# Top-k attention and an exact-GELU MLP in one kernel: an earlier first load, fewer zero products, and the first MLP block spread over two slots

## The chip, the cores and the metric

One core of one Trainium2 chip runs the whole kernel. The metric is device time in microseconds (us), the median of repeated executions. A NeuronCore has five engines that each run their own instruction stream and wait for one another through semaphores: TensorE (PE in the profile, its weight loads PEld), VectorE (DVE), ScalarE (ACT), GpSimd (POOL) and SyncE (SP, which here only issues transfers).

## The reference, cut to what matters

```python
# q, k, v: (8, 8, 576, 64) float32; w_in: (512, 2048); w_out: (2048, 512)
scores = scale * np.matmul(q, k.transpose(0, 1, 3, 2))          # scale = 1/8
kth = np.partition(scores, -top_k, axis=-1)[..., -top_k:-top_k + 1]   # top_k = 32
scores = np.where(scores >= kth, scores, -1000000000.0)
attn = np.exp(scores - scores.max(-1, keepdims=True))
attn = attn / (attn.sum(-1, keepdims=True) + 1e-09)
x = np.matmul(attn, v)        # then (B, H, S, D) -> (4608 tokens, 512)
h = x @ w_in
g = 0.5 * h * (1.0 + erf(h / sqrt(2)))
out = g @ w_out
```

For each of 64 heads, each of 576 queries keeps its 32 largest of 576 scores, a softmax over those, and the product with v. The 4608 x 512 result goes through a two-layer MLP with an exact GELU.

## The kernel before

Two heads form a pair. A pair's 576 queries are cut into 4 tiles of 128 rows and a rest of 64 rows a head. One **slot** handles one such tile for both heads; there are 144 slots and four more to drain the pipeline. The stages of a tile are spread over slots: in slot n the kernel computes the scores of tile n + 2, the top-k of tile n, the softmax of tile n - 1, the transposes of tile n - 2 and the product with v (attend) of tile n - 3. VectorE does the top-k: four rounds of MAX8 with MATCH_REPLACE8 between them, for two heads.

From slot 10 on, MLP work is put between, in **pieces**. A piece is two products of 256 columns for the first layer (l1) or one of 512 columns for the second (l2). There are 1152 pieces in all, in blocks of eight, taken in a fixed order: two l1 blocks first, then l2 and l1 blocks by turns. A Gelu for two units is due after every second block.

Setup and head:

```python
    raws = {n: [const.tile([P, NJ, 2, D], f32, name=f"raw_{n}{i}") for i in range(m)]
            for n, m in (("k", 2), ("q", 2), ("v", NP + 1))}
    for n, ts in raws.items():
        for t in ts[: 1 if n == "v" else 2]:
            (nc.vector if n == "v" else nc.gpsimd).memset(t[:, NM], 0.0)
    make_identity(nc, ident)
    for t in raws["v"][1:]:
        nc.gpsimd.memset(t[:, NM], 0.0)
    # ...
    def load(n, pair, queue=None, queue2=None):
        # ...
        for e in range(2):
            queue.dma_start(
                out=t[:, 0:NM, e, :], in_=src[b, h0 + e, 0:SM].rearrange("(t p) d -> p t d", p=P)
            )
            queue2.dma_start(out=t[e * TL : (e + 1) * TL, NM, e, :], in_=src[b, h0 + e, SM:S])
    # ... memsets of low, high and ptt on GpSimd ...
    load("k", 0, nc.scalar, nc.gpsimd)
    load("q", 0)
    load("k", 1)
    load("q", 1)
    for n in range(2):
        load_weights(FIRST + n)

    idle = raws["v"][0][:, NM].rearrange("p e d -> p (e d)")
    warm = ps.tile([P, 512], f32, tag="l1", name="warm")
    for _ in range(WARM):                 # WARM = 16
        nc.tensor.matmul(warm[:, 0:P], lhsT=idle, rhs=idle, start=True, stop=True)
    for pair in range(2):
        for piece in transpose_qk(pair, pair == 0):
            piece()
        if pair == 0:
            scores(0)
            scores(1)
```

The rows NM of each raw tile hold the last 64 rows of two heads on a diagonal; the rest of them is zero, hence the memsets. The zero products write a tile that nobody reads. Each `transpose_qk` makes three groups of transposes: k's four main blocks first, then the two last blocks of q and k, then q's four main blocks; each group is copied from PSUM to SBUF (for pair 0 the first two by VectorE, the third by ScalarE). The score tile's eviction:

```python
    def scores(i):
        # ... products into t_ps (128 columns) and s_ps (2 x 512 columns) ...
            nc.scalar.activation(spread(s, S + TL, SM), s_ps, func=AF.Copy, scale=scale)
            nc.scalar.activation(s[:, SM : S + TL], t_ps[:, 0:P], func=AF.Copy, scale=scale)
```

The slot loop:

```python
    def mlp(n):
        for _ in range(n):
            if done[0] >= len(pieces) or pieces[done[0]][0] > ready[0] or left[0] == 0:
                return
            pieces[done[0]][1]()
            done[0] += 1
            left[0] -= 1
    # ...
    for n in range(ahead):

        left[0] = 7 if START < n < START + 2 * NP else 8      # START = 10, NP = 4
        weights_add(unit_in(n))
        scores(n + 2)
        product = attend(n - 3)
        # ... mlp(1) between the softmax halves and the transposes of older tiles ...
        run_gelus()
        mlp(left[0])
        run_gelus()
        if n < N:
            top_k(n, {3: lambda: inverse(n - 1)})
        # ...
        threshold(n)
        normalise(n - 1, ...)           # on VectorE, GpSimd or both
        weights_size(unit_in(n + 1))
        # ... loads for later slots ...
```

In slots 1 to 15 and 17 a unit of weights is also rebuilt from its loaded words: ScalarE's part is `weights_size`, GpSimd's is `weights_add`. A Gelu that is due runs at the next `run_gelus()`, which stands at the end of a slot and before the first piece of each l1 unit. ScalarE needs another table for Gelu than for Exp, so each Gelu brings two table loads.

Of the kernel before, what the change touches and what calls it, by code (L numbers as in the profile page):

```python
# [14 lines left out]
def kernel(  # L15
# [19 lines left out]
    nc = tc.nc  # L35
    f32, i32, u32 = mybir.dt.float32, mybir.dt.int32, mybir.dt.uint32
    bf16, i16, u16 = mybir.dt.bfloat16, mybir.dt.int16, mybir.dt.uint16
    AF = mybir.ActivationFunctionType
    ALU = mybir.AluOpType

    B, H, S, D = q.shape
    P = 128
# [3 lines left out]
    NP = H // 2  # L46
    NM = S // P
    SM = NM * P
    TL = S - SM
# [6 lines left out]
    scale = 1.0 / float(D) ** 0.5  # L56
# [8 lines left out]
    ident = const.tile([P, P], f32, name="ident")  # L65
# [4 lines left out]

    raws = {n: [const.tile([P, NJ, 2, D], f32, name=f"raw_{n}{i}") for i in range(m)]
            for n, m in (("k", 2), ("q", 2), ("v", NP + 1))}
    for n, ts in raws.items():
        for t in ts[: 1 if n == "v" else 2]:
            (nc.vector if n == "v" else nc.gpsimd).memset(t[:, NM], 0.0)
    make_identity(nc, ident)
    for t in raws["v"][1:]:
        nc.gpsimd.memset(t[:, NM], 0.0)


    n_pairs = B * NP
# [2 lines left out]
    def raw_of(n, pair):  # L84
        return raws[n][pair % len(raws[n])]

    def load(n, pair, queue=None, queue2=None):
        if pair >= n_pairs:
            return
        queue = queue or nc.sync  # L90
        queue2 = queue2 or queue
        b, h0 = pair // NP, 2 * (pair % NP)
        t, src = raw_of(n, pair), sources[n]
        for e in range(2):
            queue.dma_start(
                out=t[:, 0:NM, e, :], in_=src[b, h0 + e, 0:SM].rearrange("(t p) d -> p t d", p=P)
            )
            queue2.dma_start(out=t[e * TL : (e + 1) * TL, NM, e, :], in_=src[b, h0 + e, SM:S])

# [20 lines left out]
    ORDER = [0, 1, 2, 3, 8, 9, 4, 5, 10, 11, 6, 7, 12, 13, 14, 15]  # L122
    FIRST = 1
    START = 2 * NP + 2
    WARM = 16
    words = {}
    low = const.tile([P, 1], f32, name="low")
    nc.gpsimd.memset(low, -EXP0 * 2.0**19)
# [51 lines left out]
    def on_pool(u):  # L180

        return SLOT_OF[u] >= START
# [3 lines left out]
    def weights_add(u):  # L186
        if u in words:
            w, _, below, d = parts(u)
            if on_pool(u):
                nc.gpsimd.tensor_scalar(  # L190
                    w.bitcast(i32), w.bitcast(u32), 2.0**-13, None, op0=ALU.mult
                )
            nc.gpsimd.tensor_tensor(d, d, below, op=ALU.add)
            nc.gpsimd.tensor_tensor(d, d, w.bitcast(i32), op=ALU.add)
        made.add(u)
# [53 lines left out]
    def spread(t, step, n):  # L249

        return bass.AP(tensor=t.tensor, offset=t.offset, ap=[list(t.ap[0]), [step, 2], [1, n]])

    def half(r, e):


        return slice((r ^ e) * TL, ((r ^ e) + 1) * TL)
# [5 lines left out]
    def scores(i):  # L262
        if i >= N:
            return
        pair, t = items[i]
        S_of[i] = s = work.tile([P, 2 * S], f32, tag="s", bufs=5, name="s")
        s_ps = ps.tile([P, 2, 512], f32, tag="s", bufs=1, name="s_ps")
        t_ps = ps.tile([P, 512], f32, tag="tp", name="t_ps")
        if t < NM:
            qk = qk_of[pair]  # L270
            lhsT = qk[:, t * P : (t + 1) * P]
            nc.tensor.matmul(t_ps[:, 0:P], lhsT=lhsT, rhs=qk[:, SM + P : KT], start=True, stop=True)  # L272
            for c in range(2):
                for e in range(2):
                    rows = slice(e * D, (e + 1) * D)
                    nc.tensor.matmul(  # L276
                        s_ps[:, e, c * 256 : (c + 1) * 256], lhsT=lhsT[rows, :],
                        rhs=qk[rows, KT + c * 256 : KT + (c + 1) * 256], start=True, stop=True,
                    )
            nc.scalar.activation(spread(s, S + TL, SM), s_ps, func=AF.Copy, scale=scale)  # L280
            nc.scalar.activation(s[:, SM : S + TL], t_ps[:, 0:P], func=AF.Copy, scale=scale)  # L281
        else:
            for r in range(2):
                qk = qk_of[pair + r]
                for e in range(2):
                    nc.tensor.matmul(
                        t_ps[half(r, e), r * TL : (r + 1) * TL],
                        lhsT=qk[:, SM + e * TL : SM + (e + 1) * TL],
                        rhs=qk[:, SM + P + e * TL : SM + P + (e + 1) * TL],
                        start=True, stop=True,  # L290
                    )

            for r in range(2):
                qk = qk_of[pair + r]
                for e in range(2):
                    rows = slice(e * D, (e + 1) * D)
                    nc.tensor.matmul(  # L297
                        s_ps[half(r, e), r, :], lhsT=qk[rows, SM + e * TL : SM + (e + 1) * TL],
                        rhs=qk[rows, KT:], start=True, stop=True,
                    )  # L300
            s2 = s.rearrange("p (r n) -> p r n", r=2)
            nc.scalar.activation(s2[:, :, 0:SM], s_ps, func=AF.Copy, scale=scale)
            nc.scalar.activation(
                s2[:, :, SM:S], t_ps[:, 0:P].rearrange("p (r n) -> p r n", r=2),
                func=AF.Copy, scale=scale,
            )
# [38 lines left out]
    def inverse(i):  # L345
        if i < 0 or i >= N:
            return
        st = stat_of[i]
        nc.vector.reciprocal(st["rden"], st["den"])  # L349

    def add_small(i):
        if i < 0 or i >= N:
            return
        st = stat_of[i]
        nc.gpsimd.tensor_scalar(st["den"], st["den"], 1e-9, None, op0=ALU.add)  # L355

    def softmax(i, e):

        if i < 0 or i >= N:
            return  # L360
        st, s = stat_of[i], row(i, e)
        nc.scalar.activation(s, s, func=AF.Prelu, bias=st["neg"][:, e, 1:2], scale=1.0, alpha=STEEP)  # L362
        nc.scalar.activation(  # L363
            s, s, func=AF.Exp, bias=st["bias"][:, e : e + 1], scale=1.0,
            accum_out=st["den"][:, e : e + 1],
        )
# [58 lines left out]
    def attend(i):  # L425
# [37 lines left out]
        if t == (NM if b % 2 == 0 else NM - 1):  # L463
            for r in range(2 if t == NM else 1):
                load("v", pair + r + NP + 1)
# [93 lines left out]
    def run_gelus():  # L559
        while waiting:  # L560
            gelus(waiting.pop(0))
# [9 lines left out]
# [9 lines that stand above are left out]
    ready, left = [0], [0]  # L580
    staging = ExitStack()
    stage = staging.enter_context(tc.tile_pool(name="stage", bufs=1))

    load("k", 0, nc.scalar, nc.gpsimd)
    load("q", 0)
    load("k", 1)
    load("q", 1)
    for n in range(2):
# [4 lines left out]
    warm = ps.tile([P, 512], f32, tag="l1", name="warm")  # L593
    for _ in range(WARM):
        nc.tensor.matmul(warm[:, 0:P], lhsT=idle, rhs=idle, start=True, stop=True)  # L595
# [19 lines left out]
    ahead = N + 4  # L615
    for n in range(ahead):

        left[0] = 7 if START < n < START + 2 * NP else 8
        weights_add(unit_in(n))
        scores(n + 2)  # L620
        product = attend(n - 3)
        late = n > START
        mlp(1)
        tr = transposes(n - 2)
        if product and n > START and done[0] < len(pieces) and pieces[done[0]][0] > ready[0]:

            for piece in tr[:1]:
                piece()
            tr, ready[0] = tr[1:], n_tok[0]
        softmax(n - 1, 0)  # L630
        mlp(1)
        if not late:
            softmax(n - 1, 1)
        mlp(1)
        prep = prep_in.pop(n, [])
        if len(prep) > 1 and len(tr) == 3:
            tr, prep = tr[:1] + prep[:1] + tr[1:], prep[1:]
        for piece in tr[:-1]:
            piece()
            ready[0] = n_tok[0]  # L640
            mlp(1)
        ready[0] = n_tok[0]
        if late:
            softmax(n - 1, 1)
        add_small(n - 1)
        for piece in tr[-1:] + prep:
            piece()
            mlp(1)
# [6 lines that stand above are left out]
        else:  # L655
            inverse(n - 1)
        threshold(n)
        u = unit_in(n + 1)

        normalise(n - 1, 0 if u not in words else 2 if on_pool(u) else 1)  # L660

        weights_size(unit_in(n + 1))
        if n >= FIRST:
            load_weights(n + 2)
        if n <= NP:
            load("v", n)
# [38 lines left out]
```

## Time and profile before

| what | value |
|---|---|
| median of 3 executions | 1654.69 us (1654.48 to 1655.39) |
| span of the profiled execution | 1653.7 us |
| TensorE busy | 1593.8 us |
| VectorE busy | 1419.6 us |
| ScalarE busy | 1184.1 us |
| GpSimd busy | 650.5 us |
| mean granted TensorE clock | 0.977 of full |
| MAX8, one instruction | 746 ns, 1152 of them |

A row of the page's second part cuts the span into 40 slices of 41 us; a digit is the busy share in tenths. In a timeline row, "xN" means that N instructions of one kind were merged; the bracket is the idle time of the engine before the row, with the instruction that ended it. A matrix product of float32 shows as two records a product, a transpose as one.

### The profile page before, as it was taken

To read this page: it belongs to the slowest core of one execution; us is meant where nothing else is said; L and a number is where in the kernel's file an instruction comes from. 1 tells how busy PE (TensorE), PEld (TensorE's weight loads), DVE (VectorE), ACT (ScalarE), POOL (GpSimd) and SP (SyncE) were. 2 spreads that over 40 slices of the span, in tenths; PEclk is the share of its full clock that TensorE was granted. 3 is DMA by queue.
4 is the path that set the end of the run, shared out by engine and by line. 5 is a ranking of instruction groups with operands and counts; after the bars stand their busy time and mean duration, and the time that the engine had idled before them with its cause. 6 is when DMAs were issued, how large, how long until landed. Compare 5 with 4: busy or idle time off the path is not lost.

```text
span 1653.7 us, 25056 instructions
## 1 busy us (share of the span) xinstructions
PE 1593.8 (96%) x8832; PEld 1080.5 (65%) x8832; DVE 1419.6 (86%) x3049; ACT 1184.1 (72%) x2131; POOL 650.5 (39%) x756
## 2 busy tenths in 40 slices
PE   6669999999999999999999999999999999999999
PEld 4346566766666667676666667676666666666665
DVE  7999899989999889998989988998889898999800
ACT  6888777777777777777777777777777777777720
POOL 3677543333333333333333333333333333333300
PEclk7669999999999999999999999999999999999999
DMA  6423210011101111011110111001110001000000
GB/s 165 139 98 102 83 43 1 14 29 29 50 1 28 30 30 28 1 28 36 29 28 1 42 29 43 1 14 28 44 35 1 27 15 34 2 14 4 4 13 13
DMA packets 126621, 56.14 MB, mean 34 GB/s; under 512 B 117760, under 2 KB 117792, under 8 KB 126496
## 3 DMA queue, kind: packets, MB, share of 16 engines
q1 hardware_dynamic: 125376, 54.25, 12.2%
q8 instruction: 70, 1.15, 0.3%
q14 instruction: 55, 0.45, 0.1%
q10 hardware_dynamic: 1056, 0.26, 0.1%
q0 software_dynamic: 64, 0.03, 0.0%
HBM read 45.08 MB, written 9.44 MB: 33 GB/s over the span
## 4 chain that ended last, share of the span: by engine, by line
PE 92%; ACT 6%; DVE 1%; issue 1%; POOL 0%; ACTq 0%; POOLq 0%; DVEq 0%
PE h_ps L495 30%; PE y_ps L531 30%; PE o L443 9%; PE s_ps L276 8%; PE tp L412 8%; PE tp_qk L231 2%; PE t_ps L272 2%; ACT s L363 1%; PE o L454 1%; ACT s L362 1%; PE s_ps L297 1%; PE tp_t L394 1%; ACT s L280 1%; POOL s L375 0%; PE warm L595 0%
## 5 line engine op out<-in xcount | busy, mean ns | idle before, releaser
L323 DVE MAX8 top<-rest 128x8 f32<-128x576 f32 x864 | 608.9, 746 | 0.0
L495 PE MATMUL h_ps<-xT,w_in_sb 128*128 128x256 f32 (+1 forms) x2560 | 554.5, 362 | 3.8 <-ACT g L506 3.8
L531 PE MATMUL y_ps<-w_out_sb,g 128*128 128x512 f32 x1152 | 549.5, 599 | 0.0
L495 PEld LDWEIGHTS h_ps<-xT,w_in_sb 128*128 128x128 f32 x2560 | 429.6, 191 | 66.6 <-issue 19.6
L375 POOL TENSOR_SCALAR s<-s,rden 128x576 f32<-128x576 f32 x266 | 456.0, 1723 | 0.8 <-issue 0.4
L326 DVE MATCH_REPLACE8 rest<-top,rest 128x576 f32<-128x576 f32 x576 | 423.0, 741 | 0.0
L355 POOL TENSOR_SCALAR den<-den 128x2 f32<-128x2 f32 x144 | 32.0, 222 | 835.2 <-ACT s L363 834.4
L531 PEld LDWEIGHTS y_ps<-w_out_sb,g 128*128 128x128 f32 x1152 | 195.1, 190 | 166.8 <-issue 165.0
L280 ACT ACTIVATE s<-s_ps 128x1024 f32<-128x1024 f32 x128 | 131.5, 1027 | 167.3 <-PE s_ps L276 149.1
L363 ACT ACTIVATE s<-s,bias 128x576 f32<-128x576 f32 x288 | 223.3, 776 | 13.3 <-ACT s L362 0.7
L362 ACT ACTIVATE s<-s,neg 128x576 f32<-128x576 f32 x288 | 223.9, 778 | 0.3 <-POOL neg L338 0.2
L419 ACT COPY pt<-tp 128x512 f32<-128x512 f32 x256 | 147.1, 574 | 103.0 <-PE tp L412 103.0
L412 PEld LDWEIGHTS tp<-ident,s 128*128 128x128 f32 x1152 | 145.9, 144 | 111.9 <-issue 59.1
L326 DVE MATCH_REPLACE8 rest<-top,s 128x576 f32<-128x576 f32 x288 | 211.6, 742 | 0.0
L323 DVE MAX8 top<-s 128x8 f32<-128x576 f32 x288 | 201.8, 742 | 3.9 <-ACT s L281 3.9
L412 PE MATMUL tp<-ident,s 128*128 128x128 f32 x1152 | 178.6, 279 | 23.6 <-ACT pt L395 22.0
L443 PE MATMUL o<-pt,raw_v 128*64 128x256 f32 x1280 | 155.5, 390 | 0.0
L276 PE MATMUL s_ps<-qk 64*128 64x256 f32 x1024 | 153.9, 421 | 0.7 <-ACT s L280 0.7
L349 DVE RECIPROCAL rden<-den 128x2 f32<-128x2 f32 x144 | 23.0, 160 | 142.1 <-POOL den L355 141.8
L443 PEld LDWEIGHTS o<-pt,raw_v 128*64 128x64 f32 x1280 | 87.8, 139 | 66.2 <-issue 23.4
L276 PEld LDWEIGHTS s_ps<-qk 64*128 64x128 f32 x1024 | 92.5, 195 | 23.7 <-issue 1.6
L506 ACT ACTIVATE g<-h_ps 128x512 f32<-128x512 f32 x144 | 78.6, 595 | 34.0 <-PE h_ps L495 33.2
(66 smaller groups left out, 1088.3 us busy)
## 6 DMA issues: line engine op xcount, KB each, us to landing
raw_q<-in_q_dram SPq DMA_DIRECT2D x64, 128.0 KB, 2.4
raw_v<-in_v_dram SPq DMA_DIRECT2D x64, 128.0 KB, 2.5
out_dram<-y SPq DMA_DIRECT2D x32, 256.0 KB, 2.1
w_out_sb<-in_moe_w_in_dram SPq DMA_DIRECT2D x16, 511.8 KB, 4.9
raw_k<-in_k_dram SPq DMA_DIRECT2D x62, 128.0 KB, 2.5
w_out_sb<-in_moe_w_out_dram SPq DMA_DIRECT2D x10, 511.8 KB, 3.9
words<-in_moe_w_out_dram SPq DMA_DIRECT2D x6, 511.8 KB, 4.5
raw_q<-in_q_dram SPq DMA_DIRECT2D x64, 16.0 KB, 2.3
```

The costliest lines, as they stand in the source:

```text
L276: nc.tensor.matmul(s_ps[:, e, c * 256 : (c + 1) * 256], lhsT=lhsT[rows, :], rhs=qk[rows, KT + c * 256 : KT + (c + 1) * 256], start=True, s ...
L280: nc.scalar.activation(spread(s, S + TL, SM), s_ps, func=AF.Copy, scale=scale)
L323: nc.vector.max(st["top"][:, e, 8 * r : 8 * r + 8], cur[e])
L326: nc.vector.match_replace(rest[:, e], st["top"][:, e, 8 * r : 8 * r + 8], cur[e], LOWEST)
L362: nc.scalar.activation(s, s, func=AF.Prelu, bias=st["neg"][:, e, 1:2], scale=1.0, alpha=STEEP)
L363: nc.scalar.activation(s, s, func=AF.Exp, bias=st["bias"][:, e : e + 1], scale=1.0, accum_out=st["den"][:, e : e + 1],)
L375: (nc.vector if e >= 2 - on_dve else nc.gpsimd).tensor_scalar(s, s, st["rden"][:, e : e + 1], None, op0=ALU.mult)
L412: nc.tensor.transpose(tp[:, j * P : (j + 1) * P], s[:, first + j * P : first + (j + 1) * P], ident)
L419: nc.scalar.copy(out=dst, in_=tp.rearrange("p (j n) -> p j n", j=NM))
L443: nc.tensor.matmul(o[e * D : (e + 1) * D, 0:n], lhsT=vt[:, j, e, :], rhs=pt[:, e * NM + j if j < NM else 2 * NM, :], start=(j == 0), stop= ...
L495: nc.tensor.matmul(h_tile(u)[:, i, :], lhsT=w_in_sb[:, ko, f * P : (f + 1) * P], rhs=xT[:, ko, c0 : c0 + n], start=(ko == 0), stop=(ko == ...
L531: nc.tensor.matmul(y_of[sub], lhsT=g_of[u][:, i, sub * P : (sub + 1) * P], rhs=w_out_sb[:, f, :], start=(f == 0), stop=(f == FT - 1),)
```

## The change

It has four parts, all at the start of the kernel.

- The first tile's rows NM of k are cleared first, by GpSimd, and the loads of k and q for pair 0 are issued right after it, before the identity is made. The other memsets of raw tiles go to VectorE. This is to have k's last rows, which GpSimd loads, in place sooner.
- Nine zero products run instead of sixteen.
- Of the first score tile, ScalarE evicts only one half of s_ps; VectorE evicts t_ps and the other half.
- Slots 10 and 11 take four MLP pieces each instead of eight and seven, and slots 12 to 17 take eight instead of seven. The first l1 block thus spans slots 10 and 11, and from slot 12 on each slot takes exactly one block.

```diff
-    for n, ts in raws.items():
-        for t in ts[: 1 if n == "v" else 2]:
-            (nc.vector if n == "v" else nc.gpsimd).memset(t[:, NM], 0.0)
-    make_identity(nc, ident)
-    for t in raws["v"][1:]:
-        nc.gpsimd.memset(t[:, NM], 0.0)
+    nc.gpsimd.memset(raws["k"][0][:, NM], 0.0)
+    for t in raws["v"][:1] + raws["q"] + raws["k"][1:] + raws["v"][1:]:
+        nc.vector.memset(t[:, NM], 0.0)
 # ... after the definition of load():
+    load("k", 0, nc.scalar, nc.gpsimd)
+    load("q", 0)
+    make_identity(nc, ident)
 # ...
-    WARM = 16
+    WARM = 9
 # ... in scores(), for a tile of 128 rows:
+            if i == 0:
+
+                nc.scalar.activation(s[:, 0:SM], s_ps[:, 0], func=AF.Copy, scale=scale)
+                nc.vector.tensor_scalar(s[:, SM : S + TL], t_ps[:, 0:P], scale, None, op0=ALU.mult)
+                nc.vector.tensor_scalar(s[:, S + TL :], s_ps[:, 1], scale, None, op0=ALU.mult)
+                return
             nc.scalar.activation(spread(s, S + TL, SM), s_ps, func=AF.Copy, scale=scale)
 # ... before the zero products:
-    load("k", 0, nc.scalar, nc.gpsimd)
-    load("q", 0)
     load("k", 1)
     load("q", 1)
 # ... at the top of the slot loop:
-        left[0] = 7 if START < n < START + 2 * NP else 8
+        left[0] = 4 if n in (START, START + 1) else 8
```

## The prediction

> **What bounds the kernel now.** I read the page first: the engine totals, the forty slices and the chain that ended last.
>
> ```profile
> PE 1593.8 (96%) x8832; PEld 1080.5 (65%) x8832; DVE 1419.6 (86%) x3049; ACT 1184.1 (72%) x2131; POOL 650.5 (39%) x756
> PE   6669999999999999999999999999999999999999
> DVE  7999899989999889998989988998889898999800
> PEclk7669999999999999999999999999999999999999
> PE 92%; ACT 6%; DVE 1%; issue 1%; POOL 0%; ACTq 0%; POOLq 0%; DVEq 0%
> ```
>
> TensorE is full from the fourth slice (41 us each) to the end, and 92% of the chain is TensorE. Only the first three slices, 0 to about 124 us, show it at 6. The last two slices are TensorE alone: MLP pieces left over after the last attention slot. So a microsecond is gained only if TensorE reaches its saturated stretch earlier with the same number of pieces done, and such a microsecond reaches the end whole.
>
> Next the timeline, first at the start and then where the Gelus run.
>
> ```profile
> 1.04 6.67 PE L595 MATMUL warm<-raw_v 128*128 128x128 f32 x32 [1.04 <-DVE raw_v L75]
> 2.73 1.26 POOL L98 DMA_DIRECT2D raw_k<-in_k_dram  x2
> 7.55 0.60 PE L231 MATMUL tp_qk<-ident,raw_k 128*128 128x128 f32 x4
> 11.86 1.02 ACT L280 ACTIVATE s<-s_ps 128x1024 f32<-128x1024 f32 x1 [1.65 <-PE s_ps L276]
> 12.78 0.27 ACT L281 ACTIVATE s<-t_ps 128x128 f32<-128x128 f32 x1
> 13.09 1.42 DVE L323 MAX8 top<-s 128x8 f32<-128x576 f32 x2 [3.88 <-ACT s L281]
> ...
> 180.77 1.74 PE L495 MATMUL h_ps<-xT,w_in_sb 128*128 128x256 f32 x4 [2.66 <-ACT g L506]
> 187.19 0.17 DVE L349 RECIPROCAL rden<-den 128x2 f32<-128x2 f32 x1 [4.04 <-POOL den L355]
> ```
>
> Columns: start, duration, engine, line, operation, and in brackets the idle time before it and what ended it. The first top-k starts at 13.09 us. From there VectorE has no idle row until slot 11: the first MAX8 of slots 1 to 11 stand at 22.74, 33.01, 43.28 and so on to 115.87 (slot 10) and 126.64 (slot 11), 10.27 us apart and 10.77 where it also does both normalisations. So the first 126 us are a VectorE chain hanging from 13.09. At 180.77 TensorE stands 2.66 us for a Gelu, and VectorE pays 4.04 us for it at 187.19.
>
> Then I cut the time at the first score product of each slot on TensorE, for slots 11 to 17.
>
> ```profile
> 127.59:137.72 10.13, 9.26 (x53) 7.46 (x52) 8.95 (x20) 9.56 (x16) 7.12 (x5) 1.00 0.67 229
> 137.72:148.51 10.79, 10.79 (x59) 6.33 (x58) 10.68 (x23) 8.73 (x16) 8.79 (x7) 1.00 0.07 22
> 148.51:160.46 11.95, 9.83 (x49) 6.62 (x47) 10.89 (x24) 11.78 (x19) 8.96 (x8) 1.00 0.18 69
> 160.46:172.45 11.99, 11.65 (x72) 7.11 (x71) 10.64 (x23) 9.12 (x17) 8.78 (x6) 1.00 0.47 138
> 172.45:187.36 14.91, 11.47 (x53) 7.25 (x53) 10.78 (x24) 12.27 (x20) 8.86 (x7) 0.89 0.37 110
> 187.36:199.15 11.79, 11.66 (x76) 7.87 (x76) 9.80 (x21) 6.84 (x15) 4.07 (x6) 1.00 0.01 1
> 199.15:206.79 7.64, 7.64 (x37) 3.75 (x38) 7.55 (x16) 7.48 (x12) 7.31 (x5) 1.00 0.35 78
> ```
>
> Columns after the stretch: its length, busy time of PE, PEld, DVE, ACT, POOL, then clock, DMA share and GB/s. Slot 15 (172.45) takes 14.91 us for 11.47 us of TensorE work, at a mean clock of 0.89. Slot 18 starts at 206.79.
>
> **What the Trainium skill says.** *TensorE: Matmul & The Clock Gate*, section "Part 1: The HAM clock gate": TensorE starts at half clock and is released after one busy window of about 3.4 us; the windows run freely, so the moment varies from run to run. The trace agrees: the sixteen zero products take 6.4 us up to the first transpose at 7.43, 0.40 us each, and the eight score records take 1.14 us at full clock (10.68) against 2.08 at half (17.87). The clock digit of the first 7 us carries no record; it isn't evidence of full clock. *ScalarE: Activation LUTs*, "What ACT_TABLE_LOAD costs": about 1.28 us for the load and 1.38 for a drain. The trace has the 1.28 (at 178.73) but the Gelu starts 0.02 us after it, so I count 1.28. *PSUM — Partial Sum Buffer*, "PSUM bank collisions raise a hardware error": two engines may read different banks at once. The two halves of s_ps are two banks, so the split of the first scores can overlap; no pair of this kind is in the trace before.
>
> **The change, part by part.**
>
> *Head.* Seven zero products less: 7 x 0.40 = 2.8 us, so the first transpose could start at 7.43 - 2.80 = 4.63. What it needs: k's main rows, issued at 0.72 and 1.24 on ScalarE's queue and landing 2.9 and 3.4 later, at 3.6 and 4.64; the identity, which now follows two DMA issues on GpSimd (1.26 us) and is there before 3. So 4.70. The second group needs q's last rows (issued 2.48, 2.7 to land: 5.2) and k's last rows: before, these were issued at 2.73 and 3.5 and landed at 6.0, which would have been the next bound; now the issue follows one memset (0.92), about 1.8 us earlier, so 4.2. Thus the zero products' 2.73 us is not taken back by a load. Moving the memsets to VectorE (seven at 0.17) costs nothing, as it stood idle to 8.18.
>
> *First scores by two engines.* Before: 1.27 us from 11.82 to 13.09 (1.02 + 0.27, overlapping a little). After: ScalarE copies 512 columns (its 128x512 copy from PSUM takes 0.585), VectorE does the 128 columns early and 512 columns in 0.69 (its own 128x512 copy at 8.18), side by side: about 0.75. Gain 0.5.
>
> Sum with full clock: 3.2 us. If the clock is still half: 3.6 us of zero products fill a freely placed 3.4 us window only sometimes, though the transposes behind them help. Then the first and third groups of four transposes cost 0.44 more each and the scores 2.78 instead of 1.56 (t_ps and s_ps at 17.17 against 10.26): 2.1 lost, gain 1.1. I give full clock 60%: 0.6 x 3.2 + 0.4 x 1.1 = 2.4 us. VectorE has no gap up to slot 10, so I carry it whole.
>
> *Slots.* Counting through the loop, before: slots 10 to 17 do 8, 7, 7, 7, 7, 7, 7, 6 pieces; after: 4, 4 and six times 8. Both stand at 56 pieces when slot 18 begins, and every later slot is the same. So the whole effect is how much earlier slot 18's first score product starts than 206.79. A piece is 0.87 us of TensorE (four h_ps records or two y_ps).
>
> Slots 10 and 11 took 112.02 to 137.72, 25.7 us. They lose 7 pieces, 6.1 us, and the Gelu after slot 10 goes behind slot 11. But VectorE needs 2 x 10.77 = 21.5, and ScalarE's order (score copy 1.3, two softmaxes 3.3, copies 2, weights 2.5) holds the last transposes. Following it by hand gives slot 12 at 133.2: 4.5 us gained.
>
> Slots 12 to 17 took 69.07 us. TensorE's own work after the change: six times scores 1.44 and transposes 1.0, three attends of 2.31, 48 pieces of 0.87 and seven q/k groups, near 65.5. Before, with 41 pieces, it is 59.4, so 9.7 us were waits: 2.66 for the Gelu in slot 15, about 1.7 for the half clock that this stop brought, the rest on ScalarE's copies. After, Gelus fall due at the ends of slots 11, 13, 15, 17, behind the slot's transposes, never before a piece that needs them in mid-slot. Walking the slots with ScalarE's loads (a Gelu slot has 1.28 x 2 + 1.1, a weight slot 2.5 more) gives starts of 147.1, 155.7, 169.9, 180.3, 192.9 and 202.4: 69.2 us, 3.7 of it waits. So +0.1.
>
> Sum: 4.5 - 0.1 = 4.4 for the slots; I take 3.9, as my walk leaves out small issue gaps of 0.24 to 0.4 us. With the head: 3.9 + 2.4 = 6.3 us. 1654.69 - 6.3 = 1648.4.
>
> **The rivals.** (a) The seven pieces moved into slots 12 to 17 are paid in full and the waits stay at 9.7: slots +6.1 against -4.5, a loss of 1.6; with the head 1653.9. For it: ScalarE is 12.27 us busy in slot 15, with no room. Against: its worst wait came from where the Gelu fell. (b) The waits nearly vanish, TensorE runs at its 65.5: slots 8.1, head 3.2, 1643.4. VectorE's floor (10.77 or 9.8 a slot, 63 us for six) would allow it; ScalarE in weight slots speaks against. (c) The head is hidden: something other than VectorE, say the first weights for ScalarE at 21.54, holds slots 1 to 10 and nothing of 2.4 arrives: 1650.8. The unbroken VectorE rows speak against. (d) Half clock through the first scores: head 1.1, 1649.7.
>
> **Range and chances.** Head 1.1 to 3.2, slots 0 to 8; both ends together are unlikely: 1644.6 to 1652.4. Two per cent is 33 us; the waits of slots 12 to 17 (9.7), the floor of slots 10 and 11 (4.5) and the head (3.2) together are about half of that. Faster by over 2%: 0.01; within: 0.98; slower: 0.01.
>
> **What would show it.** Nine zero products ending near 4.7; first transpose at 4.7 and first MAX8 at 9.9 (12.0 if half clock); slot 10's MAX8 earlier by the same amount; no 2.7 us stop for a Gelu in mid-slot and no half clock near 181; slot 18's scores at about 200.5. I am wrong if the first MAX8 moves and slot 10 doesn't, if VectorE's waits for den in slots 12 to 17 add up to 9 us again, or if the stretch from slot 18 to the end changes its length by over 1 us.

## The result, and the profile after

| kernel | median, us | ratio to the kernel before, 95% interval |
|---|---|---|
| before | 1655.12 (6 executions) | 1 |
| changed | 1647.08 (1646.13 to 1648.52, 6 executions) | 0.9952 (0.9939 to 0.9964) |

The change takes off 8.0 us, 0.5%; the prediction was 6.3. The traced execution of the changed kernel is the fastest of its six, so spans of traces differ by more than the medians: 9.3 us (1653.7 to 1644.4). The page of the changed kernel, its totals, slices, chain and two groups (after the bar: busy time and mean, then idle time before and what ended it):

```profile
PE 1593.0 (97%) x8818; PEld 1077.6 (66%) x8818; DVE 1421.3 (86%) x3058; ACT 1184.3 (72%) x2130; POOL 650.4 (40%) x749
PE   6669999999999999999999999999999999999999
DVE  7999999988898989998989898998889889999800
PEclk7669999999999999999999999999999999999999
PE 93%; DVE 4%; ACT 2%; POOL 1%; issue 0%; ACTq 0%; POOLq 0%; DVEq 0%
...
L502 PE MATMUL h_ps<-xT,w_in_sb 128*128 128x256 f32 (+1 forms) x2560 | 553.1, 361 | 1.2 <-ACT g L513 1.2
L356 DVE RECIPROCAL rden<-den 128x2 f32<-128x2 f32 x144 | 23.0, 160 | 134.9 <-POOL den L362 134.6
```

Busy times are the same within 3 us; what went is waiting. TensorE's wait for a Gelu fell from 3.8 to 1.2 us and VectorE's for den from 141.8 to 134.6. VectorE now has 4% of the chain, 1% before. The same two groups before:

```profile
L495 PE MATMUL h_ps<-xT,w_in_sb 128*128 128x256 f32 (+1 forms) x2560 | 554.5, 362 | 3.8 <-ACT g L506 3.8
L349 DVE RECIPROCAL rden<-den 128x2 f32<-128x2 f32 x144 | 23.0, 160 | 142.1 <-POOL den L355 141.8
```

The timeline at the start, and the one long wait left:

```profile
1.04 4.21 PE L600 MATMUL warm<-raw_v 128*128 128x128 f32 x18 [1.04 <-DVE raw_v L75]
1.28 1.26 POOL L95 DMA_DIRECT2D raw_k<-in_k_dram  x2 [0.35 <-POOL raw_k L73]
5.33 0.95 PE L232 MATMUL tp_qk<-ident,raw_k 128*128 128x128 f32 x4
10.00 0.60 ACT L283 ACTIVATE s<-s_ps 128x512 f32<-128x512 f32 x1 [1.65 <-PE s_ps L277]
10.63 0.69 DVE L285 TENSOR_SCALAR s<-s_ps 128x512 f32<-128x512 f32 x1 [1.41 <-ACT s L283]
11.24 1.41 DVE L330 MAX8 top<-s 128x8 f32<-128x576 f32 x2
...
189.67 0.17 DVE L356 RECIPROCAL rden<-den 128x2 f32<-128x2 f32 x1 [2.00 <-POOL den L362]
```

The first top-k comes 1.85 us earlier (13.09 to 11.24). VectorE's second copy of the first scores stands behind ScalarE's (10.63 after 10.00 + 0.60), not beside it.

Slots 11 to 17, cut at the first score product on TensorE (length, busy PE, PEld, DVE, ACT, POOL, clock, DMA share, GB/s):

```profile
123.38:131.74 8.36, 6.74 (x40) 5.25 (x38) 8.25 (x19) 7.71 (x14) 7.56 (x5) 1.00 0.65 179
131.74:145.39 13.65, 13.65 (x73) 10.30 (x74) 13.53 (x31) 13.38 (x21) 9.90 (x8) 0.87 0.29 108
145.39:155.26 9.87, 9.87 (x40) 5.07 (x38) 9.78 (x21) 8.54 (x15) 8.75 (x6) 1.00 0.25 90
155.26:167.73 12.47, 12.47 (x85) 9.27 (x84) 12.02 (x27) 11.71 (x21) 9.27 (x8) 1.00 0.43 125
167.73:178.06 10.33, 10.33 (x50) 5.10 (x49) 10.33 (x24) 8.80 (x16) 8.40 (x6) 1.00 0.19 43
178.06:190.53 12.47, 12.47 (x85) 9.28 (x84) 10.36 (x23) 10.36 (x19) 4.77 (x7) 1.00 0.29 97
190.53:199.89 9.36, 9.36 (x43) 4.51 (x42) 9.36 (x21) 8.61 (x14) 8.18 (x4) 1.00 0.28 64
```

In slots 12 to 17 the record shows no idle time of TensorE. Slot 15, which took 14.91 us before, takes 10.33. But the half clock that slot 15 had before (mean 0.89) did not go, it moved: slot 12 now has a mean of 0.87 over 13.65 us, about 3.5 us at half. Slots 10 and 11 together went from 25.70 to 20.69 us (111.05 to 131.74). Slot 18 starts at 199.89 instead of 206.79: 6.90 earlier. But the span is 9.3 us shorter, so 2.4 us came after that point.

### The profile page after: what moved, and what is told of

It reads as the page before. It is cut to its first block, busy times and chain, and to the rows that moved or that the text cites. A ratio compares the mean times of both kernels' runs of the same rounds, so it can differ in the third digit from the quotient of the medians.

```text
span 1644.4 us, 25032 instructions
## 1 busy us (share of the span) xinstructions
PE 1593.0 (97%) x8818; PEld 1077.6 (66%) x8818; DVE 1421.3 (86%) x3058; ACT 1184.3 (72%) x2130; POOL 650.4 (40%) x749
## 4 chain that ended last, share of the span: by engine, by line
PE 93%; DVE 4%; ACT 2%; POOL 1%; issue 0%; ACTq 0%; POOLq 0%; DVEq 0%
PE h_ps L502 31%; PE y_ps L538 30%; PE o L450 9%; PE s_ps L277 8%; PE tp L419 7%; DVE top L330 2%; PE tp_qk L232 2%; PE t_ps L273 2%; DVE rest L333 2%; PE o L461 1%; PE s_ps L304 1%; PE tp_t L401 1%; ACT s L370 1%; ACT s L369 1%; POOL s L382 1%; PE t_ps L293 0%
## 5 line engine op out<-in xcount | busy, mean ns | idle before, releaser
L356 DVE RECIPROCAL rden<-den 128x2 f32<-128x2 f32 x144 | 23.0, 160 | 134.9 <-POOL den L362 134.6
```

## The experiments

Eleven kernels were run besides the two, one of them twice. For the four parts of the change:

**Piece counts alone** (run twice; the trace is that of the second):

```diff
 # the kernel before
-        left[0] = 7 if START < n < START + 2 * NP else 8
+        left[0] = 4 if n in (START, START + 1) else 8
```

> The kernel before with only the piece counts changed (4 in slots 10 and 11, then 8). Theory A: VectorE's waits for den in slots 11 to 17 carry the gain; they fall from 9.4 us to about 2.2, the first top-k stays at 13.1 us, and the time falls by 7 to 7.5 us (1647.7). Rival, the prediction's own sum for this part: 3.9 us (1651.2).

> The kernel before with only the piece counts changed, again, for a trace at an undisturbed clock. From the first time of it: 1646, VectorE's waits in slots 11 to 17 near 3 us, first top-k at 12 to 13 us.

Measured: ratios 0.9942 (0.9926 to 0.9959) and 0.9938 (0.9922 to 0.9955), median 1646.1 in the second: 9 to 10 us, no less than the whole change. One execution of the first run, the traced one, took 1700.84 us at a mean clock of 0.93 and is left out of the ratio. In slots 11 to 17 VectorE's waits for den fell from 9.4 to 3.5 us (1.46 and 2.01), with the first top-k at 12.12. Theory A is right in direction only: the waits fell by 5.9 us and the time by more.

**Everything but the piece counts:**

```diff
 # the changed kernel
-        left[0] = 4 if n in (START, START + 1) else 8
+        left[0] = 7 if START < n < START + 2 * NP else 8
```

> The changed kernel with the old piece counts (8, then 7 in slots 11 to 17). Theory: the first top-k stands at 11.24 us, slot 10's is 1.85 us earlier than before, VectorE's waits stay at 9.4 us, and the time falls by about 1.9 us (1653.2). Rival: the head is hidden behind something in slots 10 to 17 and the time does not move (1655).

Measured: ratio 1.0003 (0.9994 to 1.0011), no gain. The rival holds. First VectorE's timeline around slot 11 in the kernel before, then in this one:

```profile
115.87 1.41 DVE L323 MAX8 top<-s 128x8 f32<-128x576 f32 x2
...
137.54 0.17 DVE L349 RECIPROCAL rden<-den 128x2 f32<-128x2 f32 x1 [1.17 <-POOL den L355]
```

```profile
114.34 1.42 DVE L330 MAX8 top<-s 128x8 f32<-128x576 f32 x2
125.11 1.41 DVE L330 MAX8 top<-s 128x8 f32<-128x576 f32 x2
137.35 0.17 DVE L356 RECIPROCAL rden<-den 128x2 f32<-128x2 f32 x1 [2.50 <-POOL den L362]
138.49 1.41 DVE L330 MAX8 top<-s 128x8 f32<-128x576 f32 x2
```

VectorE arrives at slot 10 1.53 us earlier and then waits 1.33 us longer, 2.50 instead of 1.17; slot 12 starts 0.19 earlier. den comes from ScalarE's softmax, and that had not moved: the softmax of tile 9 starts at 118.19 before and at 117.98 here, although what it needs from VectorE was ready about 3 and 4 us before that. ScalarE stood waiting for TensorE's product with v (tile o) just before it, here the kernel before, then this one:

```profile
117.92 0.37 ACT L448 COPY xT<-o 128x256 f32<-128x256 f32 x1 [1.80 <-PE o L443]
...
117.72 0.37 ACT L455 COPY xT<-o 128x256 f32<-128x256 f32 x1 [2.10 <-PE o L450]
```

The softmax's lead over the kernel before was still 1.43 us at 45 us. It was 0.68 behind a release of the clock (its turn from half to full) that both kernels have at 55 us, 0.28 behind the one at 75, 1.34 at 97, and 0.20 behind the one at 116. So VectorE ran unbroken to slot 11, but ahead of a slower loop of ScalarE and TensorE. The gain was spent as slack there.

**All of the first block in slot 10, none in slot 11:**

```diff
 # the changed kernel
-        left[0] = 4 if n in (START, START + 1) else 8
+        left[0] = 0 if n == START + 1 else 8
```

> The changed kernel with all eight pieces of the first block in slot 10 and none in slot 11; from slot 12 on the same pieces as in the changed kernel. Theory B, the phase: what counts is that each slot from 12 on takes exactly one block, so that Gelus fall behind a slot; VectorE's waits in slots 12 to 17 stay at 2.2 us, slot 11 gets back at most its old 1.2 us, time 1647 to 1648.5. Rival, the spread: slots 10 and 11 have to be light, the Gelu after slot 10 costs again and half of the gain (3 to 4 us) is lost, 1651.

Measured: 0.9988 (0.9980 to 0.9997), 1653.71: some 6 us lost against the changed kernel, more than the rival said; my theory of the block borders alone falls. VectorE's timeline and slots 11 and 12 cut as above:

```profile
139.02 0.17 DVE L356 RECIPROCAL rden<-den 128x2 f32<-128x2 f32 x1 [4.40 <-POOL den L362]
152.72 0.17 DVE L356 RECIPROCAL rden<-den 128x2 f32<-128x2 f32 x1 [2.83 <-POOL den L362]
```

```profile
129.32:139.20 9.88, 4.33 (x24) 3.01 (x23) 5.46 (x12) 9.53 (x16) 5.13 (x4) 0.79 0.67 229
139.20:154.13 14.93, 14.93 (x73) 10.98 (x74) 11.90 (x26) 10.05 (x17) 9.88 (x9) 0.79 0.20 71
```

Slot 10, with eight pieces and its Gelu, takes 16.10 us (15.79 before, from product to product; 12.33 in the changed kernel); slot 11 leaves TensorE only 4.33 us of work, the clock falls, and slot 12 with its eight pieces runs part of its 14.93 us at half clock (mean 0.79). The half clock across the two slots lasts about 10.3 us, against 3.4 in the changed kernel. How much of the 6 us is this and how much the Gelu of slot 10 is not separated.

**Seven pieces in slots 12 to 17:**

```diff
 # the changed kernel
-        left[0] = 4 if n in (START, START + 1) else 8
+        left[0] = 4 if n in (START, START + 1) else 7 if START < n < START + 2 * NP else 8
```

> The changed kernel with 4 pieces in slots 10 and 11 and 7 in slots 12 to 17: 50 pieces instead of 56 when slot 18 begins, lighter slots but the block borders in mid-slot. Theory B, the phase: Gelus now stand before pieces of the same slot, in slot 16 and after it in every second slot; TensorE's wait for g rises from 1.2 us to over 20 us, and the time rises to 1665 or more. Rival, the load: lighter slots 12 to 17 lose VectorE's last 2.2 us of waits, the six pieces left over cost 6 x 0.87 = 5.2 us at the end, 1650.

Measured: 1.1595 (1.1575 to 1.1614), 1919 us. Two groups of its page:

```profile
L502 PE MATMUL h_ps<-xT,w_in_sb 128*128 128x256 f32 (+1 forms) x2560 | 612.8, 385 | 188.1 <-ACT g L513 188.1
L356 DVE RECIPROCAL rden<-den 128x2 f32<-128x2 f32 x144 | 23.5, 164 | 398.6 <-POOL den L362 398.6
```

The direction of the theory was right, its size far too small: 188 us of waits for 20, 272 us of time for 18. With 50 pieces by slot 18, blocks begin two pieces before a slot's end for the rest of the kernel. A Gelu then stands before pieces of the same slot: 65 times TensorE waits, 188 us in all, and ScalarE, held up by TensorE's next scores, makes den later in turn. TensorE's own work also takes 82 us more (1675.1 us busy for 1593.0), at a mean clock of 0.946 instead of 0.976. The two make 270 of the 273 us between the spans (1917.6 and 1644.4). The kernel before allowed 57 pieces in slots 10 to 17 and did 56: the attention rows for the 57th were not there yet. That limit put the block border back at slot 18, and so probably kept such stalls out of the rest; a kernel without it was not run.

**The first scores in two PSUM tiles:**

```diff
 # the changed kernel, in scores()
+        s1_ps = ps.tile([P, 512], f32, tag="l1", name="s1_ps") if i == 0 else s_ps[:, 1]
 # ... products of the second head write s1_ps ...
-                nc.vector.tensor_scalar(s[:, S + TL :], s_ps[:, 1], scale, None, op0=ALU.mult)
+                nc.vector.tensor_scalar(s[:, S + TL :], s1_ps, scale, None, op0=ALU.mult)
```

> The changed kernel with the first score's second half in a PSUM tile of its own (an idle one of the MLP's). Theory: VectorE's copy of that half waited for ScalarE's only because both read one tile; now both run side by side and the first top-k stands at 10.6 us instead of 11.24, time lower by 0.6 (1646.5). Rival: the wait comes from the shared score tile in SBUF or from the engines themselves; first top-k stays at 11.2.

```profile
10.11 0.60 ACT L284 ACTIVATE s<-s_ps 128x512 f32<-128x512 f32 x1 [1.64 <-PE s_ps L278]
10.15 0.69 DVE L286 TENSOR_SCALAR s<-s_ps 128x512 f32<-128x512 f32 x1 [0.81 <-PE s_ps L278]
10.76 1.41 DVE L331 MAX8 top<-s 128x8 f32<-128x576 f32 x2
```

Now both copies start together, behind TensorE, and the first top-k stands at 10.76. The wait was one that the program got for a tile shared by two readers: in the changed kernel VectorE's copy waits on ScalarE's semaphore alone. The score tile in SBUF is still shared here, so that rival falls. The Trainium skill, *PSUM — Partial Sum Buffer*, "PSUM bank collisions raise a hardware error", says that reads of different banks may overlap; this timeline agrees. The time, 1646.41 (0.9938, 0.9922 to 0.9955), can't be told from the changed kernel's.

**Old order of loads, nine zero products:**

```diff
 # the changed kernel
-    nc.gpsimd.memset(raws["k"][0][:, NM], 0.0)
-    for t in raws["v"][:1] + raws["q"] + raws["k"][1:] + raws["v"][1:]:
-        nc.vector.memset(t[:, NM], 0.0)
+    # memsets, make_identity and load("k", 0), load("q", 0) where they stood before
```

> The changed kernel with the memsets, identity and loads in their old order (k's last rows late again), still nine zero products. Theory: the early load of k's last rows shares the transfer engines with k's main rows and delays these from 4.64 to 5.25 us; with the old order the first transpose stands at 4.7, k's last rows land at 6.0, and the first top-k stands at about 10.5, 0.7 us earlier than in the changed kernel. Rival, the purpose of the reorder: the second group of transposes waits for k's last rows and the first top-k stands at 11.5 or later.

Measured: first top-k at 11.18, time 1647.16 (0.9944, 0.9929 to 0.9958). Both theories miss. k's main rows landed at 5.05 us here (4.64 in the trace before, 5.25 in the changed kernel), so the first transposes start at 5.13, and the second group comes at 6.01, about when k's last rows are there. In the changed kernel the second part of these rows, issued at 2.01, took 3.4 us and landed at 5.4, not at 4.2 as the prediction had it, and the second group came at 6.12. Loading them earlier brought nothing.

**Sixteen zero products in the changed kernel:**

```diff
-    WARM = 9
+    WARM = 16
```

> The changed kernel with sixteen zero products. Theory: the first transpose stands at 7.4 us again, the first top-k at 13.1 (12.5 if the split of the first scores were worth its 0.5), and the time is 1.9 us above the changed kernel (1649). Rival: the clock is released later with nine, so sixteen lose less than 1 us.

Measured: first top-k at 11.94, time 1647.15 (0.9943, 0.9928 to 0.9957), the same. The theory misses. In this execution the clock was released at 4.6 us instead of 7.0 in the kernel before, so the last zero products ran at full clock and the first transpose came at 6.39 instead of 7.55.

**Slot 17's normalisations on VectorE, in the kernel before:**

```diff
-        normalise(n - 1, 0 if u not in words else 2 if on_pool(u) else 1)
+        normalise(n - 1, 2 if n == START + 2 * NP - 1 else 0 if u not in words else 2 if on_pool(u) else 1)
```

> The kernel before, with both normalisations at the end of slot 17 on VectorE instead of GpSimd. Theory H: TensorE's lead over VectorE at slot 18 is worth nothing, as its transposes there wait for GpSimd's normalisation (two of 1.7 us after VectorE's slot 17); with VectorE they are ready about 2.4 us earlier, TensorE's waits in slot 18 shrink from about 3 us to under 1, and the time falls by about 2.3 us (1652.8). Rival: slot 18's first score product on TensorE sets the end, as the prediction had it; the time does not move, or rises by VectorE's 0.95 us.

Measured: 0.9982 (0.9974 to 0.9990), 1652.71: about 3 us off. TensorE's first transposes in slot 18, in the kernel before and then here:

```profile
212.19 0.30 PE L399 MATMUL tp_t<-ident,s 128*64 128x128 f32 x1 [1.64 <-POOL s L375]
213.89 0.30 PE L399 MATMUL tp_t<-ident,s 128*64 128x128 f32 x1 [1.41 <-POOL s L375]
```

```profile
210.79 0.41 PE L399 MATMUL tp_t<-ident,s 128*64 128x128 f32 x2 [0.45 <-DVE s L375]
```

TensorE entered slot 18 ahead of VectorE and stood 3.05 us there for GpSimd's two normalisations, which follow VectorE's slot 17. So in the kernel before, the end hung on VectorE's end of slot 17, not on TensorE's start of slot 18. In the changed kernel this wait is 0.73 us.

**What set the pace into slot 12.** Five kernels with the new counts differ only in their heads. From each trace: the first top-k, the moment at which the clock record turns to full in slot 10, and the span.

| kernel | first top-k | clock full | span | difference |
|---|---|---|---|---|
| changed | 11.24 | 115.2 | 1644.4 | 1529.2 |
| old loads | 11.18 | 115.6 | 1644.7 | 1529.1 |
| two tiles | 10.76 | 116.3 | 1645.1 | 1528.8 |
| sixteen zero products | 11.94 | 117.2 | 1646.0 | 1528.8 |
| counts alone | 12.12 | 117.6 | 1646.5 | 1528.9 |

The moment can be read from a window across it, here of the changed kernel:

```profile
112.00:116.00 4.00, 4.00 (x22) 2.35 (x24) 3.89 (x9) 2.82 (x4) 2.74 (x3) 0.60 0.59 216
```

A mean clock of 0.60 over 4 us is 3.2 us at half and 0.8 at full, so the turn is at 115.2. The span follows that moment to 0.4 us, the first top-k only to 1.2 (span less first top-k: 1633.2 to 1634.4). The expectation below calls this turn the last release, which it isn't: in all five the clock falls once more in slot 12, 17.1 us later, for 3.4 us (132.3 to 135.7 in the changed kernel). In each of the five traces the turns up to there lie a whole number of 3.41 us apart. The Trainium skill, *TensorE: Matmul & The Clock Gate*, "Part 1: The HAM clock gate", has the windows run freely; here that turn stands at another place in each trace, 115.2 to 117.6. Five traces, one a kernel, show that the two go together, not which makes the other. To test it, TensorE was kept busy:

```diff
 # the changed kernel, in mlp()
             if done[0] >= len(pieces) or pieces[done[0]][0] > ready[0] or left[0] == 0:
+                if slot[0] <= START + 1:
+                    zeros(3)      # three products of a zero tile, read by nobody
                 return
 # ... slot[0] is the number of the slot; zeros() writes an idle PSUM tile of the MLP ...
```

> The changed kernel with three more zero products wherever a slot up to 11 finds no MLP piece to run (some 20 to 27 a slot). They compute nothing that is used; they keep TensorE busy. Theory C: up to slot 10 the loop of ScalarE and TensorE, not VectorE, sets the pace, because TensorE runs at half clock there, and the end is the moment of the last clock release (115 to 117 us) plus 1529. With the clock held, that loop gets ahead of VectorE, slot 10's first score product comes before 110 us, VectorE's waits up to slot 16 fall to 2 us or less, and the time is 1 to 2 us below the changed kernel (1645 to 1646). Rival: the half clock is harmless, the fillers only delay the transposes, time 1647 to 1649.

> The same fillers with sixteen zero products at the start. Theory C: with the clock held VectorE sets the pace, so the later first top-k (1.9 us in the trace of the changed kernel against the one before) now costs nearly its whole size, 1 to 1.9 us above the kernel with fillers and nine. Rival: the head is hidden behind something other than the clock, and the two are equal.

Measured: with nine zero products at the start 1644.21 (1643.69 to 1644.96; 0.9928, 0.9913 to 0.9943), 2.9 us below the changed kernel by medians and 1.9 below the counts alone, which ran beside it; its slowest execution is faster than every one of the five kernels without fillers (1645.58 at least). With sixteen: 1645.54 (1645.07 to 1646.18; 0.9936, 0.9921 to 0.9950). The clock slices with fillers and nine, and then a window of slots 3 to 9 in the kernel before and with fillers:

```profile
PEclk9999999999999999999999999999999999999999
```

```profile
40.00:112.00 72.00, 43.35 (x205) 27.08 (x204) 71.53 (x154) 64.21 (x106) 50.52 (x42) 0.64 0.39 123
```

```profile
40.00:112.00 72.00, 64.76 (x531) 56.53 (x529) 71.53 (x155) 65.75 (x106) 50.78 (x42) 0.98 0.40 123
```

TensorE does more useless work in these slots and the kernel is faster: the mean clock is 0.98 instead of 0.64. VectorE then waits 0.17 us in slots 10 to 17. And in this pair the head counts: the first top-k differs by 1.03 us between the two (10.98 and 12.01), the time by 1.33. One part of the expectation missed: slot 10's first score product came at 110.92, hardly earlier than 111.05. The lead comes behind it. ScalarE's wait for the product with v in slot 10, in the changed kernel and with fillers:

```profile
116.93 0.37 ACT L455 COPY xT<-o 128x256 f32<-128x256 f32 x1 [1.79 <-PE o L450]
...
114.75 0.37 ACT L455 COPY xT<-o 128x256 f32<-128x256 f32 x1 [1.09 <-PE o L450]
```

The softmax behind it starts at 115.02 instead of 117.20. The gain in time lies in slot 10 (10.69 us instead of 12.33) and slot 12 (12.99 instead of 13.65), where TensorE ran part of its MLP pieces, scores and attends at half clock before. Fillers with the old counts were not run, so what the head is worth there with the clock held stays open.

**All together:** fillers, two tiles, slot 17's normalisations on VectorE.

> The changed kernel with the fillers, the first score's second half in its own PSUM tile, and slot 17's normalisations on VectorE. If the theories hold, their parts add: from the kernel with fillers (1644.2) the split gives 0.5, as VectorE now carries the head to the end, and the normalisation up to 0.7, TensorE's wait left in slot 18: 1643.0 to 1643.7. If TensorE's saturated stretch begins elsewhere, no gain over 1644.2.

Measured: 1643.99 (1642.87 to 1644.32; 0.9931, 0.9917 to 0.9944), the same as with fillers alone. The first top-k came at 10.59 and TensorE had no wait at the start of slot 18, but slot 12 took 14.2 us instead of 13.0 and VectorE waited 1.46 us in slot 16. The parts don't add, and the trace shows where they went:

```profile
92.21 0.52 DVE L383 TENSOR_SCALAR s<-s,rden 128x576 f32<-128x576 f32 x1 [0.48 <-PE s_ps L278]
133.95 1.25 ACT L175 ACTIVATE w_in_sb<-w_out_sb,low 128x1024 int32<-128x1024 int16 x1 [1.09 <-DMA w_out_sb<-in_moe_w_in_dram]
137.61 0.33 PE L402 MATMUL tp_t<-ident,s 128*128 128x128 f32 x1 [0.93 <-ACT s L289]
```

VectorE lost its lead of 0.39 us in a wait of 0.48 before slot 8: that slot's first MAX8 stands at 92.64, with fillers alone at 92.67. In slot 12 ScalarE stood 1.09 us for a transfer of weight words, and TensorE in turn 0.93 us for ScalarE. That made slot 12 1.22 us longer; slot 18 became 0.92 us shorter (11.72 instead of 12.64). Whether each execution has the late transfer, one trace can't say.

## Why the prediction was right, and which steps failed

The total, 6.3, is near 8.0 in part by luck: two errors had opposite signs. A head worth nothing was counted as 2.4 us, and piece counts worth 9 to 10 us were counted as 3.9.

- **"VectorE has no gap up to slot 10, so I carry it whole"**: failed. The head was sized at 2.4 and measured 1.85 at the first top-k, but with the old counts it is worth nothing (1.0003), and with the new ones the old head does as well. What failed is the path: VectorE has no gap, but den, which it needs at the end of slot 11, comes from a loop of ScalarE and TensorE that runs in part at half clock, and this loop set the pace into slot 12. With the clock held its softmax came 2.2 us earlier. Rival (c) was the right one, with another cause than the weights it named.
- **Zero products, 2.73 us**: k's main rows landed at 5.25 instead of 4.64 and the first group ran at half clock, which leaves 1.85 (2.73 less 0.6 and 0.28). The 4.64 came from one trace, and it was the earliest landing in thirteen.
- **Scores by two engines, 0.5 us**: 0.0, because of the wait inside one tile (1.24 us from the start of ScalarE's copy to the first top-k, 1.23 before); with two tiles 0.65.
- **Slots 10 and 11, 4.5 us**: 5.0. **Slots 12 to 17, +0.1**: -0.9 (68.15 us instead of 69.07). The walk by hand held in its sum but not in its parts: it has 3.7 us of waits where the record shows none, and it doesn't have the half clock in slot 12. The Gelu stall and the half clock near 181 us went as said. By the yardstick of the prediction, TensorE's start of slot 18, the sum of 6.3 compares with 6.90.
- **"The whole effect is how much earlier slot 18's first score product starts"**: failed. TensorE came to slot 18 early and waited there for normalisations. That wait fell from 3.05 to 0.73 us, another 2.3. So the slots' term, 3.9, was mis-sized: alone they bring 9 to 10 us.
- **Range and chances**: every execution of the changed kernel lies inside the range, and 0.5% is within 2%. The stretch from slot 18 to the end did change by more than 1 us, one of the signs named as proof against the sum.

## What to carry to other kernels

An engine without idle time need not be the bound. It isn't if what it waits for next is made by a slower loop with slack in between, so look at when its results are used. Where work is dealt out in fixed portions, see where the block borders fall; block borders two pieces before a slot's end cost 272 us here against the changed kernel. An engine whose clock falls when its load is light may be worth keeping busy with useless work before the dense part begins; here that brought 1.9 to 2.9 us.

## What the runs showed that I had not expected

- 468 more TensorE records (9286 against 8818) made the kernel 1.9 to 2.9 us faster.
- The end of the kernel followed the moment of one clock release to 0.4 us over the traces of five kernels.
- Two engines reading two halves of one PSUM tile ran one after the other (1.41 us idle on VectorE); with two tiles they started within 0.04 us.
- The second half of k's main rows, a transfer of 128 KB issued at 1.24 us, took anywhere from 3.4 to 4.2 us to land over thirteen traces.
